# A scan and two MLPs on one core: running products stored ahead of block 1's rows and decays, rows in runs of 4 KB, GpSimd without splits and low parts

## The chip, the cores and the metric

The kernel runs on one core of a Trainium2 chip. A core has a matrix engine (TensorE, PE in the views), three engines for elementwise work (VectorE = DVE, ScalarE = ACT, GpSimd = POOL), a queue engine that issues DMA transfers (SyncE = SP), and 16 DMA engines that carry them. Each engine runs its own instructions in the order in which they are written and waits on semaphores for the others. The metric is the device time of one execution in microseconds (us); lower is better.

## The reference

A chunked linear scan (attention-like, with decays) feeds two MLPs one after the other. Shapes: 4 sequences, 8 heads, 768 positions, head width 32, state 16; the result is read as 3072 tokens of width 256, and both MLPs go from 256 to 2048 and back.

```python
# scan, for every chunk of positions
la = log(clip(a, 1e-6, 1));  cum = cumsum(la)
y  = ((C B^T) * exp(cum_i - cum_j) * causal) x  +  (C state) * exp(cum)
state = exp(sum(la)) * state + sum_j exp(cum_last - cum_j) B_j x_j
# first MLP, weights w_in, w_out
h = x @ w_in;  g = max(h, 0) + log1p(exp(-abs(h)));  x = g @ w_out
# second MLP
h = x @ w_in;  g = h if h >= 1, 0 if h <= -1, else (h + 1)^2 / 4;  out = g @ w_out
```

The weights of the MLPs come in 64-bit floats and the result is in 32-bit floats.

## The kernel before, in words

**Tiling.** The scan is cut into 6 chunks of 128 positions, called blocks 0 to 5, and each block into 4 units, one for each sequence: 24 units, u = 4c + b. A block of 4 units is 512 tokens, and one block is the moving side of the MLPs' products. A step s of the first MLP takes one slice of 128 hidden features (`fc`) of one block: `up` multiplies the block by the slice of w_in, ScalarE's softplus makes g from it, and `down` multiplies g by the slice of w_out into a running sum. Steps 0 to 3 take half a block and two slices each. Two consecutive slices need one piece of each weight: i2, o2 are the pieces of steps 4 and 5, i3, o3 those of 6 and 7, i4, o4 those of 8 and 9, and so on.

**Split numbers.** TensorE multiplies rounded 32-bit numbers quickly and unrounded ones slowly. So most factors are split into a high part (a cast, line 722) and a low part (the rest, by a subtraction: `split_w` at line 955 for weights, `g_lo` at 1424 for g). `up` makes three products for each of two halves of the depth (high x high, high x low, low x high: lines 1314 to 1316), `down` six for two output halves (1450). The first steps (`s < WHOLE`) are "whole": their `down` multiplies g and the weight unsplit (1438), and needs no `g_hi` and no `g_lo`, but takes TensorE longer for each product.

**Weights.** A piece of a 64-bit weight is 512 KB. It is loaded (`load_w`, line 769) into one of four buffers, and put together to 32 bits: `w0` and `w1` on ScalarE (785, 793; `w0` now and then on VectorE, 781), `w2` and `w3` on VectorE (805, 817), then the cast (722 or 724) and the subtraction (955).

**Decays.** For block 0 they are made by products. For blocks 1 to 5 the clipped `a` is stored once to DRAM (`clip_z`), and `rows` reads each pair of units back, broadcast to 128 partitions (line 1080, two transfers of 256 KB for a pair); VectorE's scan along the row then forms the running products (`decay`, line 1110). A second scan (`runs`, 1054) gives the running products from the start of each chunk. `store_runs` writes them to DRAM, one transfer for each block (1059), and `dec` reads a block's back, broadcast to 128 partitions (1087, 256 KB), for VectorE's multiplications (`cd`, 1130).

**What sets the order.** All of this is written as jobs with needs, costs for each engine that may run them, and buffers taken and given. A planner, `Jobs.order`, walks through time, gives each job to the engine on which it would end first (plus `BIAS`), sets the jobs of an engine one after another by due time, and has `RUSH` to shift single due times. Transfers are planned with a common pipe of `RATE` bytes per ns, and VectorE and GpSimd with a lock, since both are taken to hold each other up. The program then writes every engine's instructions in that order, so a change of a constant can move instructions everywhere. SyncE issues all transfers of this part of the program, one after another.

The scan's own products (lines 1152, 1201, 1223, 1255) stand between the steps of the first MLP, up to about 140 us; the second MLP ends the program.

Of the kernel before, what the change touches and what calls it, by code (L numbers as in the profile page):

```python
# [27 lines left out]
class Jobs:  # L28
# [18 lines left out]
    def order(self, slots, begin):  # L47
# [53 lines left out]
        for _ in range(len(jobs)):  # L101
            best = []
            for name in ready:
                options, _, _, takes, _, _ = jobs[name]
                got = pick(takes, min(at[name].values()))
                if got is None:
                    continue
                starts = {e: max(got[0], at[name][e], clock[e]) for e in options}
                bias = lambda e: BIAS_2 if e == POOL and name[0] == "split_w" and name[1] else BIAS.get(e, 0)
                _, start, engine = min((starts[e] + cost + bias(e), starts[e], e) for e, cost in options.items())  # L110
                best.append((start, due[name], number[name], name, engine, got[1]))
            assert best, [(name, jobs[name][3]) for name in ready]
# [13 lines left out]
            kind = name if isinstance(name, str) else name[0]  # L126
            if engine == POOL:

                begun = start + 60
                for a, b in locked:  # L130
                    if a < begun + cost and b > begun:
                        begun = b
                shared = [name, begun, begun + cost]
                cost += begun - start
            elif engine == DVE and kind in LOCKED:
                if shared and start < shared[2] and start + cost > shared[1]:
                    if start <= shared[1]:
                        late = start + cost - shared[1]
                        shared[1] += late
                        shared[2] += late  # L140
                        clock[POOL] = self.done[shared[0]] = shared[2]
                        self.end[shared[0]] += late
                        for other in after[shared[0]]:
                            if other in at:
                                for e in at[other]:
                                    at[other][e] = max(at[other][e], shared[2] + (80 if e == POOL else self.LATENCY[POOL]))
                    else:
                        cost += shared[2] - start
                locked = locked[-20:] + [(start, start + cost)]
# [90 lines left out]
def program():  # L240
# [30 lines left out]
        add(("rows_of", b), {DVE: 210, ACT: 200}, needs=["terms"] + [("columns", 1), ("rows_of", b - 1)] * (b == NB - 1), gives=["terms"] * (b == NB - 1))  # L271
    add("clip_load", SP, 400, due=-1e5, size=98e3)
    add("clip", DVE, 350, needs=["clip_load", ("columns", 1)] + [("rows_of", b) for b in range(NB - 1)])
    add("store", SP, 800, needs=["clip"], size=98e3)
    add("runs", DVE, 1500, needs=["clip", ("columns", 1)] + RUNS)
    for c in range(1, NC):
        add(("store_runs", c), SP, 600, needs=["runs"], size=16e3)
        add(("dec", c), SP, 400, needs=[("store_runs", i) for i in range(1, NC if c == 2 else 2)], takes=["dec"], size=262e3)
    for u in range(NU):
        c, b = divmod(u, NB)  # L280
        if u % 2 == 0:
# [2 lines left out]
        if c == 0:  # L284
            for hg in range(2):
                add(
                    ("spread", u, hg), PE, 470, needs=[("columns", hg), ("rows_of", u)] + ([("spread", u, 0)] if hg else []),
                    takes=[("acc", "h")] + [("ld", "lp")] * (hg == 0),
                )
                add(("decay", u, hg), ACT, 520, needs=[("spread", u, hg)], gives=[("part", ("spread", u, hg), 0)])  # L290
            decay = [("decay", u, 0), ("decay", u, 1)]
        else:
            if b % 2:
                add(("rows", u), SP, 1100, needs=["store"], takes=["lp"], size=524e3)
            add(("decay", u), DVE, 1130, needs=[("rows", pair_of(u))])
            decay = [("decay", u)]
            add(("cd", u), DVE, 200, needs=[("load", u), ("dec", c)])
# [79 lines left out]
    for m in range(2):  # L377
        for j in sorted(range(8), key=lambda j: first_use[m, j]):
            for kind in "io":
# [18 lines left out]
                w_made = ("s_sum", j) if m and kind == "i" else ("w2" if signed(*w) else "w3", *w)  # L398
                add(("w_hi", *w), {ACT: 520, DVE: 350}, needs=[w_made])
                if m == 0:  # L400
                    add(("split_w", *w), {DVE: 610, POOL: 1300}, needs=[("w_hi", *w)])
                    continue
                add(("w_lo", *w), DVE, 610, needs=[("w_hi", *w)])
                add(("put_w", *w), SP, 800, needs=[("w_lo", *w)], gives=[("w0", *w)] * (kind == "o"), size=524e3)
# [21 lines left out]
    for k, (m, p) in enumerate(GROUPS):  # L426
        done = finished(2 * p, 2 * p + 1) if m else [("ready", NU - 1)]
        done += [
            [], [("spill", i) for i in range(3)], [("p4", NFC * NC // 4 - 1)],
            [("fill", i) for i in range(3)],  # L430
        ][k]
        t = [("t_sum", k, i) for i in range(4)]
        sums = lambda n: {POOL: 1400 * n} if k in T_POOL else {DVE: 610 * n}
        add(t[0], sums(4), needs=done, takes=["w32"] * 3)
        add(t[2], sums(1), needs=[t[0]])
        add(t[1], sums(1), needs=[t[2]])
        add(t[3], sums(2), needs=[t[1], ("t_lo", k, 2)])
        for i in range(4):
            add(("t_hi", k, i), {POOL: 700, ACT: 520}, needs=[t[i]])
            add(  # L440
                ("t_lo", k, i), {POOL: 1500, DVE: 610}, needs=[("t_hi", k, i)] + [("t_lo", k, h) for h in (0, 1, 2) if i == 3],
                gives=[t[0]] * (i == 3),
            )


    for s, (m, c, t0, n, fc, m_fc) in enumerate(steps):
# [44 lines left out]
        if whole(s):  # L491
            needs = [("g", s)] + before + [("w2" if signed(0, "o", j) else "w3", 0, "o", j) for j in pieces]
            gives = [("g", s)]
        else:
            add(("g_hi", s), {ACT: 520, DVE: 360}, needs=[("g", s)], takes=["gh"])
            add(("g_lo", s), {DVE: 610, POOL: 1300} if s < GL_POOL else {DVE: 610}, needs=[("g_hi", s)], takes=["gl"], gives=[("g", s)])
            needs = [("g_lo", s)] + before + [("split_w", m, "o", j) for j in pieces]
            gives = [("g_hi", s), ("g_lo", s)]
        first = fc == 0 and t0 == 0
# [21 lines left out]


ORDER = [(0, 0, 0, 4), (0, 1, 0, 4), (0, None, 4, 12), (1, None, 0, 16)]
WHOLE = 8
ACT_UNTIL = 96
H_MORE = 16
H_ALL = 84
GL_POOL = 16
COLD = 0.0
KEEP = 26000.0  # L530
SIGNAL = 55.0
# [9 lines left out]
PRELU = (2, 2)  # L541
LOW_ACT = 1
PRE_FROM = 3
BIAS = {DVE: 400, POOL: 500}
PATIENCE = 0
EARLY = 30000.0
HASTE = 0
STAND_BY = 400
FAR = 10000.0
CHUNK = 9  # L550
BIAS_2 = 9000
RATE = 330.0
BEGIN = 14000.0
STRETCH = 1.0
LEAD = 2
# [10 lines left out]
N_G = 3  # L566
BEHIND = 500.0
RUSH = {
    ("decay", 2, 1): -8000, ("decay", 5): -16000, ("load_w", 1, "i", 2): -16000, ("w3", 0, "o", 4): 8000,
}  # L570
WARM = 10

# [5 lines left out]
def tile_kernel(ctx: ExitStack, tc: tile.TileContext, a0, al, bc, ub, w_in, w_out, w2_in, w2_out, out):  # L578
# [129 lines left out]
        return unit(*t_at[k][2 * (i - 1) + lo])  # L708


    clip_z = dram.tile([NU, 2, H * HALF], F32, name="clip_z")
    pre_w = {
        (kind, j, lo): dram.tile([128, 512], F32, name=f"pre_{kind}{j}{lo}") for kind in "io" for j in range(8) for lo in range(2)
    }
# [322 lines left out]
    def store(engine, *step):  # L1037
# [5 lines left out]
                queue = nc.scalar if len(parts_of) > 1 and i == 0 else nc.sync  # L1043
                queue.dma_start(out[steps[s][1], e, :, i * n:i * n + n], part[:, 0:n])
        else:
            nc.sync.dma_start(clip_z.rearrange("u s (h i) -> (u s) h i", h=H), z_t)

    @job
    def runs(engine):
# [5 lines left out]

    @job
    def store_runs(engine, c):
        n = NB * 2
        nc.sync.dma_start(clip_p[c].rearrange("h r i -> r h i"), tiles["clip"][c * n:(c + 1) * n])

    @job
    def load_bc(engine, v):
# [12 lines left out]
    @job  # L1075
    def rows(engine, u):

        t = flat(buf(*got["rows", u][0])).rearrange("p (u f) -> p u f", u=2)
        for s in range(2):
            nc.sync.dma_start(  # L1080
                t[s * HALF:(s + 1) * HALF], clip_z[u - 1:u + 1, s].unsqueeze(0).to_broadcast([HALF, 2, H * HALF])
            )

    @job
# [500 lines left out]
```

## Time and profile before

| | us |
|---|---|
| three runs | 555.36, 555.64, 560.16 |
| median | 555.64 |
| profiled execution | 557.88 |
| its span | 556.2 |
| granted TensorE clock in it | 1.00 (full) |

The profiled execution is one execution of its own, with the profiler on; its time is 1.7 us longer than its span, which runs from the first to the last instruction. The page and the answers that were read of it are shown further below. In a timeline the instructions of one engine overlap a little, since the next is begun before the last has ended: a "0.68" that is followed by another start 0.60 later takes 0.60 of the engine. "out<-in" gives the tile written and the tile read by the program's names, and a name after "<-" in brackets is the work whose end released the waiting instruction. A DMA share of 1 is all 16 DMA engines busy.

### The profile page before, as it was taken

The numbers are of one execution on the slowest core, as the hardware profiler recorded it, in microseconds if no ns is written. First come the engines' busy times: TensorE is split into PE (matmuls) and PEld (weight loads), VectorE is DVE, ScalarE is ACT, GpSimd is POOL, SyncE is SP. The second block draws the span as 40 slices with busy tenths as digits, with TensorE's granted clock in tenths as the row PEclk, the third lists the DMA queues.
The fourth block names the chain that finished last, engine by engine and source line by source line (L and its number), as shares of the span: only waits on it lengthen the run. The fifth ranks groups of instructions, "written<-read, shape, count | busy, mean of one in ns | idle before, by whom it ended". The sixth has DMA issues, their size and how long they took to land.

```text
span 556.2 us, 10449 instructions
## 1 busy us (share of the span) xinstructions
PE 546.8 (98%) x3994; PEld 442.3 (80%) x3994; DVE 435.7 (78%) x813; ACT 391.7 (70%) x720; POOL 39.2 (7%) x45
## 2 busy tenths in 40 slices
PE   9898999999999999999999999999999999999997
PEld 4765878878888888888888788888888888888885
DVE  6987999888865989876777898989886665876663
ACT  7968646645455666766566989786987875888773
POOL 3112220000000100001300000021310000000000
PEclk9999999999999999999999999999999999999999
DMA  8985467576242500276436314514100001100002
GB/s 280 392 220 178 138 194 210 165 235 183 93 165 75 180 1 1 96 258 205 143 113 214 128 59 152 171 56 130 62 1 0 1 1 38 39 0 1 1 1 76
DMA packets 34679, 64.73 MB, mean 116 GB/s; under 512 B 3684, under 2 KB 8164, under 8 KB 34628
## 3 DMA queue, kind: packets, MB, share of 16 engines
q1 hardware_dynamic: 34484, 63.93, 35.3%
q8 instruction: 31, 0.51, 0.4%
q14 instruction: 20, 0.16, 0.1%
q10 hardware_dynamic: 144, 0.13, 0.1%
HBM read 47.61 MB, written 16.43 MB: 115 GB/s over the span
## 4 chain that ended last, share of the span: by engine, by line
PE 87%; DMA 8%; DVE 2%; ACT 1%; SPq 1%; issue 1%; DVEq 0%; ACTq 0%
PE acc L1450 44%; PE h L1321 5%; PE h L1323 5%; PE h L1322 5%; PE z L1321 4%; PE z L1323 4%; PE z L1322 4%; PE h L1314 3%; PE h L1315 3%; PE h L1316 3%; DMA raw<-in_w_out_dram 2%; DMA ld<-clip_z 2%; DMA dec<-clip_p 2%; PE y L1223 1%; DMA st<-in_w_out_dram 1%; DMA u<-in_ub_dram 1%
## 5 line engine op out<-in xcount | busy, mean ns | idle before, releaser
L1424 DVE TENSOR_TENSOR gl<-g,gh 128x512 fp32r<-128x512 f32 x181 | 127.6, 709 | 55.1 <-PE acc L1450 31.0
L1450 PE MATMUL acc<-gh,woh 128*128 128x512 f32 x368 | 144.3, 392 | 0.0
L1450 PE MATMUL acc<-gh,wol 128*128 128x512 f32 x368 | 143.3, 389 | 0.0
L722 ACT CAST gh<-g 128x512 fp32r<-128x512 f32 x172 | 106.8, 621 | 26.4 <-PE acc L1450 14.2
L1450 PE MATMUL acc<-gl,woh 128*128 128x512 f32 x368 | 113.6, 389 | 0.0
L1450 PEld LDWEIGHTS acc<-gh,woh 128*128 128x128 f32 x368 | 69.1, 188 | 15.2 <-issue 0.5
L1450 PEld LDWEIGHTS acc<-gl,woh 128*128 128x128 f32 x368 | 69.1, 188 | 14.4
L1450 PEld LDWEIGHTS acc<-gh,wol 128*128 128x128 f32 x368 | 69.1, 188 | 14.1
L1409 ACT ACTIVATE g<-h 128x512 f32<-128x512 f32 x61 | 36.4, 597 | 51.7 <-PE h L1316 36.6
L1401 ACT ACTIVATE t<-t 128x512 f32<-128x512 f32 x96 | 60.9, 634 | 1.9
L1314 PE MATMUL h<-xh,wih 128*128 128x512 f32 (+1 forms) x114 | 46.0, 403 | 0.5 <-ACT wih L722 0.5
L1315 PE MATMUL h<-xh,wil 128*128 128x512 f32 (+1 forms) x114 | 42.9, 376 | 0.7 <-DVE wil L955 0.7
L1316 PE MATMUL h<-xl,wih 128*128 128x512 f32 (+1 forms) x114 | 42.9, 376 | 0.0
L1110 DVE TENSOR_TENSOR_SCAN ld<-ld,eye_t 128x512 f32<-128x512 f32 x20 | 25.1, 1289 | 4.0 <-DMA ld<-clip_z 2.7
L1394 ACT ACTIVATE t<-h 128x512 f32<-128x512 f32 x37 | 22.1, 598 | 7.8 <-PE h L1323 6.7
L1314 PEld LDWEIGHTS h<-xh,wih 128*128 128x128 f32 x114 | 21.4, 188 | 6.2 <-issue 1.1
L1413 DVE TENSOR_TENSOR g<-h,t 128x512 f32<-128x512 f32 x37 | 25.3, 685 | 1.1 <-ACT t L1401 0.3
L1394 ACT ACTIVATE t<-z 128x512 f32<-128x512 f32 x35 | 21.0, 599 | 7.1 <-DVE g L1413 3.9
L1315 PEld LDWEIGHTS h<-xh,wil 128*128 128x128 f32 x114 | 21.5, 188 | 5.6 <-DVE wil L955 1.0
L1413 DVE TENSOR_TENSOR g<-z,t 128x512 f32<-128x512 f32 x35 | 24.0, 686 | 1.5 <-ACT t L1401 0.5
L1316 PEld LDWEIGHTS h<-xl,wih 128*128 128x128 f32 x114 | 21.4, 188 | 4.0
L1409 ACT ACTIVATE g<-z 128x512 f32<-128x512 f32 x19 | 11.4, 598 | 17.4 <-PE z L1316 8.8
(320 smaller groups left out, 1008.0 us busy)
## 6 DMA issues: line engine op xcount, KB each, us to landing
st<-in_w_in_dram SPq DMA_DIRECT2D x15, 512.0 KB, 5.9
st<-in_w_out_dram SPq DMA_DIRECT2D x15, 512.0 KB, 6.7
u<-in_ub_dram SPq DMA_DIRECT2D x24, 256.0 KB, 6.2
ld<-clip_z SPq DMA_DIRECT2D x20, 256.0 KB, 6.0
bc<-in_bc_dram SPq DMA_DIRECT2D x12, 384.0 KB, 6.5
pre_i<-st_plain SPq DMA_DIRECT2D x15, 256.0 KB, 2.0
pre_s<-st_plain SPq DMA_DIRECT2D x14, 192.0 KB, 5.5
pre_o<-st_plain SPq DMA_DIRECT2D x10, 256.0 KB, 3.7
```

What stands on the lines that cost most here:

```text
L722: nc.scalar.copy(out, in_)
L1314: nc.tensor.matmul(o, wh, xh[c][:, k, t0:t0 + n], start=(k == 0), stop=False)
L1315: nc.tensor.matmul(o, wl, xh[c][:, k, t0:t0 + n], start=False, stop=False)
L1316: nc.tensor.matmul(o, wh, xl[c][:, k, t0:t0 + n], start=False, stop=(k == 1))
L1321: nc.tensor.matmul(bank, wh, bh, start=start, stop=False, skip_group_check=True)
L1322: nc.tensor.matmul(bank, wl, bh, start=False, stop=False, skip_group_check=True)
L1323: nc.tensor.matmul(bank, wh, bl, start=False, stop=True, skip_group_check=True)
L1401: nc.scalar.activation(out=t, in_=t, func=AF.Square, scale=0.5 / SAT, bias=0.5)
L1409: nc.scalar.activation(out=g, in_=ph, func=AF.Softplus)
L1413: nc.vector.tensor_tensor(out=g, in0=ph, in1=t, op=ALU.max)
L1424: engines[engine].tensor_tensor(out=mine("g_lo", s)[0], in0=mine("g", s)[0], in1=mine("g_hi", s)[0].bitcast(F32), op=ALU.subtract)
L1450: nc.tensor.matmul(acc_t(s, e), w, g[:, j * n:(j + 1) * n], start=(begins(e, j) and g is gh and i == 0), stop=(fc + j == NFC - 1 and g is ...
```

## The change

- `WHOLE` goes from 8 to 6: steps 6 and 7 are split like all later ones, with `g_hi` and `g_lo` jobs of their own.
- GpSimd no longer gets subtractions of the kinds `split_w`, `g_lo` and `t_lo`, nor casts `t_hi` (the set `POOLED` is empty). 25 jobs leave it: 5 `split_w`, 3 `g_lo` and 12 `t_lo` go to VectorE, 5 `t_hi` to ScalarE. With the `g_lo` of steps 6 and 7, VectorE has ten subtractions more in the first 100 us.
- `clip_z` is laid out so that the two units of a pair lie behind each other; each partition's row is read as one piece of 4 KB instead of two of 2 KB. `COPIES = 1` keeps one copy.
- `store_runs` is two transfers for each block instead of one, ten in all instead of five.
- The planner's costs and rates for `rows`, `store_runs` and `dec` grow, its lock is modelled otherwise, and `RUSH` has other entries.

The core of the diff:

```diff
-                bias = lambda e: BIAS_2 if e == POOL and name[0] == "split_w" and name[1] else BIAS.get(e, 0)
+                bias = lambda e: BIAS.get(e, 0)
...
-                begun = start + 60
-                for a, b in locked:
-                    if a < begun + cost and b > begun:
-                        begun = b
-                shared = [name, begun, begun + cost]
+                begun = max([b for a, b in locked if a < start + 60 < b], default=start + 60)
+                shared = [name, begun, begun + cost, False]
...
-    add("store", SP, 800, needs=["clip"], size=98e3)
+    add("store", SP, 400 * COPIES, needs=["clip"], size=98e3 * COPIES)
...
-        add(("store_runs", c), SP, 600, needs=["runs"], size=16e3)
-        add(("dec", c), SP, 400, needs=[("store_runs", i) for i in range(1, NC if c == 2 else 2)], takes=["dec"], size=262e3)
+        add(("store_runs", c), SP, 700, needs=["runs"], size=16e3)
+        add(("dec", c), SP, 400, needs=[("store_runs", i) for i in range(1, NC if c == 2 else 2)], takes=["dec"], size=262e3 * 1.5)
...
-                add(("rows", u), SP, 1100, needs=["store"], takes=["lp"], size=524e3)
+                add(("rows", u), SP, 1100, needs=["store"], takes=["lp"], size=524e3 * SLOW)
...
-                    add(("split_w", *w), {DVE: 610, POOL: 1300}, needs=[("w_hi", *w)])
+                    add(("split_w", *w), {POOL: 1300} if ("split_w", *w) in POOLED else {DVE: 610}, needs=[("w_hi", *w)])
...
-            add(("t_hi", k, i), {POOL: 700, ACT: 520}, needs=[t[i]])
+            add(("t_hi", k, i), {ACT: 520}, needs=[t[i]])
...
-            add(("g_lo", s), {DVE: 610, POOL: 1300} if s < GL_POOL else {DVE: 610}, needs=[("g_hi", s)], takes=["gl"], gives=[("g", s)])
+            add(("g_lo", s), {POOL: 1300} if ("g_lo", s) in POOLED else {DVE: 610}, needs=[("g_hi", s)], takes=["gl"], gives=[("g", s)])
...
-WHOLE = 8
+WHOLE = 6
...
-BIAS = {DVE: 400, POOL: 500}
+BIAS = {DVE: 600}
+POOLED = set()
...
-BIAS_2 = 9000
-RATE = 330.0
+RATE = 370.0
+COPIES = 1
+SLOW = 1.75
...
-    ("decay", 2, 1): -8000, ("decay", 5): -16000, ("load_w", 1, "i", 2): -16000, ("w3", 0, "o", 4): 8000,
+    ("decay", 2, 1): -4000, ("decay", 5): -16000, ("load", 17): 8000, ("rows", 9): -4000, ("w0", 0, "i", 4): 16000,
...
-    clip_z = dram.tile([NU, 2, H * HALF], F32, name="clip_z")
+    clip_z = dram.tile([COPIES, 2, NU, H * HALF], F32, name="clip_z")
...
-        n = NB * 2
-        nc.sync.dma_start(clip_p[c].rearrange("h r i -> r h i"), tiles["clip"][c * n:(c + 1) * n])
+        for s in range(2):
+            r = s * NU + c * NB
+            nc.sync.dma_start(clip_p[c].rearrange("h (b s) i -> s b h i", s=2)[s], tiles["clip"][r:r + NB])
...
-                t[s * HALF:(s + 1) * HALF], clip_z[u - 1:u + 1, s].unsqueeze(0).to_broadcast([HALF, 2, H * HALF])
+                t[s * HALF:(s + 1) * HALF].rearrange("p u f -> p (u f)"),
+                clip_z[:, s, u - 1:u + 1].rearrange("k u f -> k (u f)").unsqueeze(1).to_broadcast(
+                    [COPIES, HALF // COPIES, 2 * H * HALF]
+                ),
```

The order moves at three places. On SyncE, from o4's weight to the decays (`st_136` to `st_139` are the four weight buffers, `ld_121` and `ld_122` the rows of two pairs, `dec_134` and `dec_135` the two decay slots), before:

```order
L769 DMA st_139<-in_w_out_dram 128x2x512
L1080 DMA ld_122<-clip_z 64x2x512 x2
L1080 DMA ld_121<-clip_z 64x2x512 x2
L1059 DMA clip_p<-more_148 8x8x64 x5
L769 DMA st_136<-in_w_in_dram 128x2x512
L769 DMA st_137<-in_w_out_dram 128x2x512
L769 DMA st_138<-in_w_in_dram 128x2x512
L1087 DMA dec_134<-clip_p 128x1x512
L1087 DMA dec_135<-clip_p 128x1x512
L769 DMA st_139<-in_w_out_dram 128x2x512
```

and with the change:

```order
L1079 DMA ld_122<-clip_z 64x1x1024 x2
L1079 DMA ld_121<-clip_z 64x1x1024 x2
L1058 DMA clip_p<-more_148 4x8x64 x2
L766 DMA st_139<-in_w_out_dram 128x2x512
L1058 DMA clip_p<-more_148 4x8x64 x8
L766 DMA st_136<-in_w_in_dram 128x2x512
L766 DMA st_138<-in_w_out_dram 128x2x512
L1089 DMA dec_134<-clip_p 128x1x512
L1089 DMA dec_135<-clip_p 128x1x512
L766 DMA st_137<-in_w_in_dram 128x2x512
L766 DMA st_139<-in_w_out_dram 128x2x512
```

The load of o4 stood ahead of the rows and now stands behind them and two of the ten stores; i6, which stood ahead of both decays, now stands behind them, and the second decay is block 3's.

On ScalarE, around the rebuild of i5 and the steps behind it (lines 793 and 790 are `w1`, 785 and 782 `w0`, 722 and 719 the cast, 1409 and 1411 the softplus; names `g` and `gh` are reused buffers), before:

```order
L722 CAST woh_93<-w_482 128x512
L1409 ACTIVATE gh<-h_208 128x512
L722 CAST wih_78<-w_566 128x512
L722 CAST woh_94<-w_586 128x512
L1409 ACTIVATE gh<-h_210 128x512
L793 ACTIVATE t<-st_136,low_bias 128x512
L785 ACTIVATE w_566<-st_136 128x512
L793 ACTIVATE t<-st_137,low_bias 128x512
L785 ACTIVATE w_586<-st_137 128x512
L1409 ACTIVATE gh<-h_208 128x512
L793 ACTIVATE g<-st_138,low_bias 128x512
```

and with the change:

```order
L790 ACTIVATE t<-st_136,low_bias 128x512
L719 CAST wih_78<-w_545 128x512
L1411 ACTIVATE g<-h_210 128x512
L790 ACTIVATE g<-st_138,low_bias 128x512
L719 CAST gh<-g 128x512
L782 ACTIVATE w_603<-st_138 128x512
L719 CAST woh_94<-w_603 128x512
L1411 ACTIVATE g<-h_208 128x512
L719 CAST gh<-g 128x512
L790 ACTIVATE t<-st_137,low_bias 128x512
L1411 ACTIVATE g<-h_210 128x512
L782 ACTIVATE w_669<-st_137 128x512
```

The cast of `wih_78`, the weight piece i4 of steps 8 and 9, stood ahead of the rebuild of `st_136` and now stands behind its `w1`. The g of step 6 goes to `g`, with a cast to `gh`, and that cast stands behind the `w1` of o5 (`st_138`).

On TensorE, the end of step 7's `up` and what follows it (`h` is the bank of `up`, `acc` the running sums), before:

```order
L1316 MATMUL h_208<-xl_360,wih_77 128x512
L1438 MATMUL acc_285<-gh,w_482 128x512
L1438 MATMUL acc_270<-gh,w_482 128x512
L1314 MATMUL h_210<-xh_359,wih_78 128x512
L1315 MATMUL h_210<-xh_359,wil_86 128x512
L1316 MATMUL h_210<-xl_360,wih_78 128x512
L1314 MATMUL h_210<-xh_359,wih_78 128x512
L1315 MATMUL h_210<-xh_359,wil_86 128x512
L1316 MATMUL h_210<-xl_360,wih_78 128x512
L1438 MATMUL acc_285<-gh,w_482 128x512
L1438 MATMUL acc_270<-gh,w_482 128x512
```

and with the change:

```order
L1318 MATMUL h_208<-xl_360,wih_77 128x512
L1316 MATMUL h_210<-xh_359,wih_78 128x512
L1317 MATMUL h_210<-xh_359,wil_86 128x512
L1318 MATMUL h_210<-xl_360,wih_78 128x512
L1316 MATMUL h_210<-xh_359,wih_78 128x512
L1317 MATMUL h_210<-xh_359,wil_86 128x512
L1318 MATMUL h_210<-xl_360,wih_78 128x512
L1452 MATMUL acc_285<-gh,woh_93 128x512
L1452 MATMUL acc_285<-gh,wol_101 128x512
L1452 MATMUL acc_270<-gh,woh_93 128x512
L1452 MATMUL acc_270<-gh,wol_101 128x512
```

Step 8's `up` (with `wih_78`) stood behind the whole down of step 6 and now stands ahead of that down, which is split.

## Rows read from the trace of the kernel before

**Rows 1.** The page, part 1: busy us, share of the span, instructions.
```profile
PE 546.8 (98%) x3994; PEld 442.3 (80%) x3994; DVE 435.7 (78%) x813; ACT 391.7 (70%) x720; POOL 39.2 (7%) x45
```

**Rows 2.** Stretches: length, busy PE, PEld, DVE, ACT, POOL; PEclk, DMA share, GB/s.
```profile
100.00:160.00 60.00, 60.00 (x1100) 48.59 (x1099) 52.28 (x117) 32.05 (x67) 0.00 (x0) 1.00 0.55 172
...
300.00:540.00 240.00, 239.83 (x1058) 198.12 (x1057) 183.58 (x298) 193.94 (x344) 12.18 (x10) 1.00 0.15 52
```

**Rows 3.** Waits of TensorE, 0 to 100 us: total, times, longest.
```profile
PE acc L1438 <- ACT gh L1409: 2.1, 2, 1.5
...
PE y L1223 <- DVE ld L1166: 0.8, 1, 0.8
```

**Rows 4.** Timeline of TensorE: start, us, instruction, [idle before <- releaser].
```profile
33.69 1.88 PE L1438 MATMUL acc<-gh,w 128*128 128x512 f32 x4
...
35.63 0.39 PE L1315 MATMUL h<-xh,wil 128*128 128x512 f32 x1
...
39.90 1.88 PE L1438 MATMUL acc<-gh,w 128*128 128x512 f32 x4
...
43.72 1.98 PE L1438 MATMUL acc<-gh,w 128*128 128x512 f32 x4 [0.55 <-ACT gh L1409]
...
47.63 0.50 PE L1314 MATMUL h<-xh,wih 128*128 128x512 f32 x1 [0.53 <-ACT wih L722]
48.78 0.50 PE L1315 MATMUL h<-xh,wil 128*128 128x512 f32 x1 [0.66 <-DVE wil L955]
```

**Rows 5.** The chain of waits, 0 to 80 us: start, us, what.
```profile
3.48 5.80 DMA st<-in_w_in_dram
...
26.32 9.42 DMA ld<-clip_z
...
55.74 1.36 PE acc L1450 x6
```

**Rows 6.** Timeline of SyncE's queue: issue, us, transfers.
```profile
9.30 0.37 SPq L769 DMA_DIRECT2D raw<-in_w_out_dram  x1
...
34.25 0.41 SPq L769 DMA_DIRECT2D st<-in_w_in_dram  x1
35.13 0.40 SPq L769 DMA_DIRECT2D st<-in_w_out_dram  x1
35.81 0.37 SPq L769 DMA_DIRECT2D st<-in_w_in_dram  x1
```

**Rows 7.** Timeline of VectorE.
```profile
45.42 0.90 DVE L1130 TENSOR_TENSOR u<-u,dec 128x128 f32<-128x128 f32 x4 [4.70 <-DMA dec<-clip_p]
```

**Rows 8.** Timeline of ScalarE.
```profile
37.94 0.76 ACT L793 ACTIVATE t<-st,low_bias 128x512 uint32<-128x512 uint32 x1 [0.35 <-DMA st<-in_w_in_dram]
...
41.88 0.76 ACT L793 ACTIVATE t<-st,low_bias 128x512 uint32<-128x512 uint32 x1 [2.61 <-DMA st<-in_w_out_dram]
```

**Rows 9.** Stretches about the rows and dec.
```profile
22.00:28.00 6.00, 6.00 (x44) 5.73 (x43) 5.83 (x8) 5.35 (x13) 1.56 (x2) 1.00 1.05 389
28.00:33.40 5.40, 5.40 (x26) 4.60 (x25) 4.17 (x9) 4.29 (x8) 1.42 (x1) 1.00 1.04 219
41.00:45.50 4.50, 3.95 (x13) 2.00 (x11) 0.08 (x1) 3.48 (x6) 0.00 (x0) 1.00 0.80 218
```

**Rows 10.** VectorE by line, 0 to 100 us: busy us, mean ns | idle before.
```profile
L1110 DVE TENSOR_TENSOR_SCAN ld<-ld,eye_t 128x512 f32<-128x512 f32 x12 | 15.6, 1341 | 2.4 <-DMA ld<-clip_z 2.4
L805 DVE SCALAR_TENSOR_TENSOR w<-w,t 128x512 uint32<-128x512 uint32 x13 | 9.9, 759 | 2.0 <-ACT w L785 1.2 <-ACT w L783 0.4 <-ACT t L793 0.2
L1424 DVE TENSOR_TENSOR gl<-g,gh 128x512 fp32r<-128x512 f32 x10 | 7.8, 790 | 0.2 <-ACT gh L722 0.2
L817 DVE SCALAR_TENSOR_TENSOR w<-st,w 128x512 uint32<-128x512 uint32 x10 | 7.7, 781 | 0.0
...
L955 DVE TENSOR_TENSOR wil<-w,wih 128x512 fp32r<-128x512 f32 x7 | 4.8, 682 | 0.0
```

**Rows 11.** The page, part 5: the scan over the whole span.
```profile
L1110 DVE TENSOR_TENSOR_SCAN ld<-ld,eye_t 128x512 f32<-128x512 f32 x20 | 25.1, 1289 | 4.0 <-DMA ld<-clip_z 2.7
```

More of the change, by code (lines that the diff above doesn't have):

```diff
@@ L136, in order @@
                 if shared and start < shared[2] and start + cost > shared[1]:
-                    if start <= shared[1]:
+                    if start <= shared[1] and not shared[3]:
                         late = start + cost - shared[1]
-                        shared[1] += late
-                        shared[2] += late
+                        shared[1:] = shared[1] + late, shared[2] + late, True
                         clock[POOL] = self.done[shared[0]] = shared[2]
@@ L438, in program @@
         for i in range(4):
-            add(("t_hi", k, i), {POOL: 700, ACT: 520}, needs=[t[i]])
+            add(("t_hi", k, i), {ACT: 520}, needs=[t[i]])
             add(
-                ("t_lo", k, i), {POOL: 1500, DVE: 610}, needs=[("t_hi", k, i)] + [("t_lo", k, h) for h in (0, 1, 2) if i == 3],
+                ("t_lo", k, i), {POOL: 1300} if ("t_lo", k, i) in POOLED else {DVE: 610}, needs=[("t_hi", k, i)] + [("t_lo", k, h) for h in (0, 1, 2) if i == 3],
                 gives=[t[0]] * (i == 3),
@@ L527 @@
 H_ALL = 84
-GL_POOL = 16
 COLD = 0.0
@@ L1045, in store @@
         else:
-            nc.sync.dma_start(clip_z.rearrange("u s (h i) -> (u s) h i", h=H), z_t)
+            for i in range(COPIES):
+                nc.sync.dma_start(clip_z[i].rearrange("s u (h i) -> (s u) h i", h=H), z_t)
     @job
@@ L1551 @@
     c6 = C.reshape(NB, H, NC, Q, N)
-    al = np.ascontiguousarray(a.reshape(NB, H, NC, 2, HALF).transpose(2, 0, 3, 1, 4)).reshape(NC * NB * 2, H * HALF)
+    al = np.ascontiguousarray(a.reshape(NB, H, NC, 2, HALF).transpose(3, 2, 0, 1, 4)).reshape(NC * NB * 2, H * HALF)
     a0 = np.ascontiguousarray(a6[:, :, 0]).reshape(NB * H, Q)
```

## The prediction, made before the changed kernel was run

> **What bounds the kernel now.** The busy line comes first: TensorE works 98% of the span [rows 1]. A mean over a span hides stages, so the second view is the table of stretches [rows 2]: TensorE is busy in every microsecond from 100 to 160 us and in 239.83 of 240 from 300 to 540, at the full granted clock, while VectorE (183.58 of 240) and ScalarE have room. Time can only be won there by giving TensorE less to do, or in the first 100 us by removing its waits. The list of waits of that stretch [rows 3] has 2.1 us for g from ScalarE and 0.8 for ld from VectorE, and its timeline [rows 4] shows 0.53 and 0.66 more at 47.63 and 48.78 us. That is 4.1 us of waits for what the change moves. With the matmuls that it saves (0.7, below), 4.8 us could be won in all. A measurement of this kernel can tell about 1% from no change, 5.6 us, so a gain that large is nearly excluded before anything is costed. A loss isn't: every new wait in this dense stretch counts in full.
>
> The chain of waits [rows 5] and SyncE's timeline [rows 6] show what feeds the stretch. The weight of 3.48 us lands at 3.48 + 5.80 = 9.28, and the ninth transfer issued from it on is issued at 9.30. Likewise the block-1 rows hold the queue: the last of four lands at 26.32 + 9.42 = 35.74 and the next issue begins at 35.81. I read this as eight transfers outstanding on SyncE, the next waiting for the oldest.
>
> **The change part by part.** *Whole downs.* Steps 6 and 7 lose the four unsplit products. From the start at 33.69 to the product at 35.63 is 1.94 us; less the 0.23 of the product between, a whole down takes 1.71. A split one takes 1.36 [rows 4, 5]. Two steps: 2 x (1.71 - 1.36) = **-0.7 us**.
>
> *Waits that go.* VectorE sits 4.70 us before its first multiplication by dec [rows 7], and behind it stand the rebuild of block weights and the subtractions that TensorE waits for at 43.72, 47.63 and 48.78: 0.55 + 0.53 + 0.66 [rows 4]. In the new order those weights stand elsewhere, so I drop all three: **-1.7 us**. Bounds: 0 if they only change place, -2.5 if ld's 0.8 [rows 3] goes too.
>
> *Rows in runs of 4 KB, with o4's weight behind them.* (iN and oN are pieces N of the first MLP's two weights.) Without that weight's 512 KB ahead the rows land 0.5 / 0.389 = 1.3 us sooner, near 34.4. For the length of the runs two rows give bounds: 389 GB/s while weights and other loads are moved, 219 while rows are mainly moved [rows 9]. 1 MB takes 2.7 us at the one and 4.8 at the other, so longer runs are worth 0 to -2.1 us of landing time. I take 0: both stretches have runs of 2 KB or thereabouts, so it is the source, one short tensor read 64 times, that differs. The Trainium skill (DMA: Bandwidth & Descriptors, Specifications) asks for at least 512 B per transfer for full rate; by that, 2 KB was long enough and 4 KB brings nothing. The trace agrees that run length alone isn't the price, with 389 against 219 at equal runs. The scan at 35.99 isn't what TensorE waits for, so sooner rows buy TensorE nothing directly.
>
> *What the queue then does.* This is the new cost. Ten stores of running products stand where five did, with o4's weight after the second. The tenth store is the eighth issue behind that weight, and so waits for its landing: 1.3 us behind the rows at 34.4 gives 35.7 to 35.9. The weight i5 is issued at 36.3 instead of 34.25 [rows 6]. Before, it was used at 37.94 less the 0.09 of handing over: 3.6 us after issue [rows 8]. So it lands at 39.9. ScalarE then rebuilds it (0.67 to the next instruction) and only then casts the weight of step 8 (0.62), which the new order puts behind it. Step 8's first product, now ahead of down 6 and so due at 39.90 [rows 4], starts at 41.2: **1.3 us**, and 0.4 more before its second product, which needs VectorE's 0.61 subtraction behind the cast: 1.7. Bounds 0 (weight as early as before) and 2.4 (o4 lands only when the rows did before). Down 6 then needs g_hi, behind o5's rebuild on ScalarE. That weight took 41.8 - 35.1 = 6.7 us [rows 6, 8]; issued at 36.7 it is there at 43.4, the cast ends 43.4 + 0.67 + 0.62 = 44.7, and step 8's products end near 44.4: **0.3**; upper bound 1.2, when dec, which one multiplication ahead of g_lo 6 on VectorE waits for, arrives at 45.42 as before. Last, i6 is fetched behind both decs, and ScalarE's rebuild of it stands ahead of the g of the step after: **1.0**, an estimate by half of what dec keeps VectorE waiting less two steps of cover (4.70/2 - 1.36); bounds 0 and 2.0. Together **+3.0**, from 0 to +5.6.
>
> *GpSimd gives its splits away.* Before 100 us VectorE takes ten more subtractions of 0.61 (its steps apart; 682 ns each with overlap): 6.1 us. Against it stands what sharing with GpSimd cost: the twelve scans of L1110 took 1341 ns, all twenty 1289, so the other eight (20 x 1289 - 12 x 1341) / 8 = 1211; the low parts of g (L1424) 790 against the 682 of L955, the two rebuilds 759 and 781 against the same [rows 10, 11]. 12 x 0.13 + 10 x 0.11 + 13 x 0.08 + 10 x 0.10 = 4.7 us. The 1.4 left over I cost at **0**: VectorE's 4.70 us before dec [rows 7] hide it; without that cover it is 1.4. GpSimd itself is in no wait of rows 3 and 4. The later low parts, twelve of 0.61 on VectorE and five casts on ScalarE, lie where VectorE has 56 of 240 us free: 0, with 7.3 us of VectorE as the price if it were full.
>
> Sum: -0.7 - 1.7 + 3.0 = **+0.6 us**. The profiled run took 557.88 us (span 556.2), so 558.5 for it; it lies 2.24 over the median of the runs, which I take as scatter. Against the median, 555.64 + 0.6 = **556.2 us**.
>
> **The rivals.**
> *A. The weights come in time.* If rows land at the lower bound (-2.1), o4, i5 and what follows are issued as early as before, and the new waits vanish. For it: nothing in the rows says that the 219 is the source rather than the runs. Against it: the queue order. Gain 0.7 + 1.7 = 2.4, with ld's 0.8 gone 3.2: 552.4 to 553.2, **552.8**. Chance 0.25.
>
> *B. The decs block more than I charge.* The window before dec's arrival at 45.4 moves 218 GB/s at a DMA share of 0.80 [rows 7, 9]. If both decs use half the DMA engines, 256 KB cost 1.35 us each instead of 0.67, i6 is held longer, and down 8 waits at its upper bound: +2.5 to +4.9, **559 to 560.5**. The share of 0.80 speaks against it, because half the engines would show 0.5, unless another transfer fills the others. Chance 0.15. The Trainium skill (DMA: Bandwidth & Descriptors, Why a DMA increments its semaphore by 16 and not by 1) has the transfer spread over the largest divisor, up to 16, of the slowest dimensions; dec's source has 8 heads outermost, which would make it 8.
>
> *C. The other side: 4 KB reads of the same 4 KB are slower, not faster.* All 64 partitions read one line; if longer pieces collide more and a block's rows take 8 us instead of the 5.4 of 28.00 to 33.40, VectorE's scans, which already wait 2.4 us for clip_z [rows 10], stand in blocks 1 to 5, some 1.5 to 2 us each: 555.64 + 0.6 + 6 to 9 = **562 to 565**. It decides from a transfer of about 8 us on, where cover in the dense stretch (VectorE 52.28 of 60) runs out. Chance 0.07.
>
> *D. The change doesn't do what it says:* the decay fetched "sooner" is issued at 37 us after all, behind ten stores. This is inside my forecast.
>
> **How the numbers follow.** Forecast 0.53, A 0.25, B 0.15, C 0.07. Predicted is the forecast's 556.2. The range takes the forecast with all bounds: low -0.7 - 1.7 - 0.8 + 0 = -3.2, 552.5; high -0.7 + 0 + 5.6 = +4.9, 560.5. It covers A and B and leaves C out. Faster by over 1% (below 550.1) needs more than the waits there are: 0.03, for something not in these rows. Slower by over 1% (above 561.2) is C and a little of B's end: 0.10. Within 1%: 0.87.
>
> **What would show it.** Right: SyncE's issue of i5 near 36.3 instead of 34.25; a wait before step 8's first product of over 1 us, with ScalarE's cast as releaser; no wait of L1438 at 43; VectorE's L1110 at 1.21 instead of 1.34 us; rows landing at 34 or later. Wrong: rows landing near 32 (A), a wait of VectorE on clip_z of more than 5 us (C), idle of TensorE behind 100 us from VectorE's or ScalarE's new low parts, which I cost at nothing, or a granted clock below 1.00.

## The result, and the profile after

The changed kernel took 560.14 us (median of 16 runs), the kernel before 557.20 (16 runs, its first three among them): a ratio of 1.0052, 95% interval 1.0033 to 1.0071, which is 2.9 us more (1.8 to 4.0). That lies within 1%, inside the range, and above the 556.2 that I had forecast, or 557.8 if the forecast's +0.6 is set on the median of 557.2.

The profiled execution took 560.20 us, its span is 558.5. The page's first line, as in [rows 1]:

```profile
PE 548.1 (98%) x4000; PEld 443.2 (79%) x4000; DVE 437.8 (78%) x827; ACT 397.4 (71%) x735; POOL 5.8 (1%) x20
```

TensorE is as full as before. GpSimd's 39.2 us are 5.8. The waits of TensorE in the first 100 us, as in [rows 3]:

```profile
PE y L1159 <- DMA bc<-in_bc_dram: 2.5, 1, 2.5
PE acc L1452 <- ACT gh L719: 1.3, 1, 1.3
...
PE acc L1452 <- DVE gl L1426: 0.4, 1, 0.4
PE acc L1440 <- ACT gh L1411: 0.3, 1, 0.3
```

None of the waits that I took away is left: no whole down (L1438, now L1440) waiting at 43 us, no wih, no wil, no ld. But the longest one is new and stands where I had looked at nothing: 2.5 us at 5 to 8 us, for bc, the B and C of the first units. The stretches behind it (columns as in [rows 2]):

```profile
8.00:10.00 2.00, 2.00 (x18) 0.90 (x14) 0.00 (x0) 0.00 (x0) 0.00 (x0) 0.57 0.97 349
10.00:12.00 2.00, 2.00 (x7) 0.93 (x6) 0.60 (x1) 1.21 (x3) 0.42 (x2) 0.57 1.06 407
```

After that wait the granted clock is 0.57 for 4 us: for most of them TensorE runs at the lower of its two levels, 1.2 GHz. Up to the issue of bc at 2.08 us SyncE does the same in both kernels, and this has to be put aside before anything else can be read from the two traces; the first two experiments do that.

SyncE's queue, as in [rows 6]:

```profile
27.30 2.55 SPq L1058 DMA_DIRECT2D clip_p<-more  x2
30.94 0.41 SPq L766 DMA_DIRECT2D st<-in_w_out_dram  x1
32.09 5.12 SPq L1058 DMA_DIRECT2D clip_p<-more  x8
37.32 0.40 SPq L766 DMA_DIRECT2D st<-in_w_in_dram  x1
...
39.69 0.38 SPq L766 DMA_DIRECT2D st<-in_w_in_dram  x1
```

In both kernels the stores stand behind block 1's rows and ahead of the decays; the title has them ahead of the rows, which they are not. o4's weight is issued at 30.94, eight more stores hold the queue for 5.12 us, and i5 goes out at 37.32 instead of 34.25. Behind both decays i6 follows at 39.69, where it was 35.81. VectorE's work by form, as in [rows 10]:

```profile
L1112 DVE TENSOR_TENSOR_SCAN ld<-ld,eye_t 128x512 f32<-128x512 f32 x12 | 14.1, 1211 | 0.4 <-DMA ld<-clip_z 0.2
L1426 DVE TENSOR_TENSOR gl<-g,gh 128x512 fp32r<-128x512 f32 x16 | 11.0, 685 | 1.7 <-ACT gh L719 1.6
L802 DVE SCALAR_TENSOR_TENSOR w<-w,t 128x512 uint32<-128x512 uint32 x11 | 7.6, 687 | 1.3 <-ACT w L780 0.7 <-ACT w L782 0.6
```

The scan takes 1211 ns instead of 1341, the low parts 685 instead of 790, the rebuild 687 instead of 759, the figures from which I had costed GpSimd's part.

### The profile page after: what moved, and what is told of

It reads as the page before. It is cut to its first block, busy times and chain, and to the rows that moved or that the text cites. A ratio compares the mean times of both kernels' runs of the same rounds, so it can differ in the third digit from the quotient of the medians.

```text
span 558.5 us, 10424 instructions
## 1 busy us (share of the span) xinstructions
PE 548.1 (98%) x4000; PEld 443.2 (79%) x4000; DVE 437.8 (78%) x827; ACT 397.4 (71%) x735; POOL 5.8 (1%) x20
## 4 chain that ended last, share of the span: by engine, by line
PE 91%; DMA 3%; ACT 3%; DVE 2%; issue 1%; SPq 1%; ACTq 0%
PE acc L1452 44%; PE h L1323 5%; PE h L1324 5%; PE h L1325 5%; PE z L1323 4%; PE z L1324 4%; PE z L1325 4%; PE h L1316 4%; PE h L1317 4%; PE h L1318 4%; DMA st<-in_w_in_dram 2%; PE y L1225 1%; PE acc L1440 1%; DMA bc<-in_bc_dram 1%; PE y L1257 1%; PE z L1317 1%
## 5 line engine op out<-in xcount | busy, mean ns | idle before, releaser
L1452 PE MATMUL acc<-gh,woh 128*128 128x512 f32 x372 | 146.1, 393 | 1.3 <-ACT gh L719 1.3
L1452 PE MATMUL acc<-gh,wol 128*128 128x512 f32 x372 | 144.9, 389 | 0.0
L719 ACT CAST gh<-g 128x512 fp32r<-128x512 f32 x175 | 108.6, 620 | 25.3 <-PE acc L1452 15.2
L1452 PE MATMUL acc<-gl,woh 128*128 128x512 f32 x372 | 114.9, 389 | 0.4 <-DVE gl L1426 0.4
L1112 DVE TENSOR_TENSOR_SCAN ld<-ld,eye_t 128x512 f32<-128x512 f32 x20 | 23.5, 1211 | 1.3 <-DMA ld<-clip_z 1.1
```

The source lines that it names most:

```text
L719: nc.scalar.copy(out, in_)
L1452: nc.tensor.matmul(acc_t(s, e), w, g[:, j * n:(j + 1) * n], start=(begins(e, j) and g is gh and i == 0), stop=(fc + j == NFC - 1 and g is ...
```

## The experiments

Ratios are to the kernel before, run on the same chip in turn with each kernel; one per mille is 0.56 us. e1 and e2 are single runs and have no ratio.

| kernel | ratio | 95% interval |
|---|---|---|
| the change | 1.0052 | 1.0033 to 1.0071 |
| e3 stores late, o4 early | 1.0050 | 1.0031 to 1.0070 |
| e4 before + whole layout | 1.0037 | 1.0023 to 1.0051 |
| e5 ScalarE's order | 1.0050 | 1.0033 to 1.0066 |
| e6 before + 4 KB runs, five stores | 0.9990 | 0.9970 to 1.0010 |
| e7 before + ten stores | 1.0026 | 1.0013 to 1.0039 |
| e8 before, GpSimd freed | 1.0062 | 1.0045 to 1.0078 |
| e9 the change, five stores | 1.0002 | 0.9986 to 1.0019 |
| e10 e9 + second decay late | 1.0001 | 0.9986 to 1.0016 |
| e11 e10 + ScalarE's order | 0.9987 | 0.9971 to 1.0004 |

### Both kernels again (e1, e2)

No edit. Expected of the kernel before:

> The kernel before, unchanged, for a second trace. Scatter theory: the late landing of the first bc (7.69 us in the changed kernel's trace, 5.30 in this one's, with the same instructions up to it) is a matter of the single execution, and can show here as well; then TensorE waits up to 2.5 us for bc at 5 to 8 us. Change theory: here it lands near 5.3 us again.

and of the changed one:

> The changed kernel, unchanged, for a second trace. Scatter theory: the first bc lands near 5.3 us in this execution or another; then the queue's delay (i5 issued at 36 to 37 us) is no longer covered by a late start, and TensorE's waits between 40 and 52 us grow to 3 us or more. Change theory: bc lands near 7.7 us again, the granted clock falls to 0.57 in 8 to 12 us, and the waits stay at some 2 us.

TensorE's waits of the kernel before, first 100 us of this execution:

```profile
PE acc L1438 <- ACT gh L1409: 2.0, 1, 2.0
...
PE y L1223 <- DVE ld L1166: 0.8, 1, 0.8
PE h L1315 <- DVE wil L955: 0.7, 1, 0.7
PE y L1157 <- DMA bc<-in_bc_dram: 0.3, 1, 0.3
PE h L1314 <- ACT wih L722: 0.2, 1, 0.2
```

and of the changed kernel:

```profile
PE h L1316 <- ACT g L1411: 1.9, 1, 1.9
PE y L1225 <- DVE ld L1168: 1.3, 1, 1.3
...
PE acc L1440 <- ACT gh L1411: 0.4, 1, 0.4
```

bc is waited for 0.3 us in the one and not at all in the other. So the 2.5 us are not in every execution of the change. Over all the traces of this study that wait is none and 0.3 us in the two of the kernel before, 0.4 and 0.2 in e6 and e8, which are made from it and keep its five stores, 0.7, 1.8 and 1.1 in e9 to e11, and 2.5, none, 0.3, 0.9, 1.4 and 1.0 with ten stores (the change, e2, e3, e4, e5, e7). Of the last nine only e2 and e3 wait as little as the first four, so a part of the late start may go with the kernel; thirteen traces can't settle it. The 16 runs of each kernel spread over 4.8 and 3.6 us. Why the landing varies is open.

These two make a clean pair: spans of 555.4 and 557.3, 1.9 us apart. With the start undisturbed, the wait that I had predicted is there; at 1.9 us it is shorter than the 3 us expected of e2. TensorE in the changed kernel (timeline, as in [rows 4]):

```profile
42.50 0.50 PE L1316 MATMUL h<-xh,wih 128*128 128x512 f32 x1 [1.87 <-ACT g L1411]
...
43.50 0.63 PE L1316 MATMUL h<-xh,wih 128*128 128x512 f32 x1
```

and ScalarE beside it:

```profile
40.70 0.76 ACT L790 ACTIVATE t<-st,low_bias 128x512 uint32<-128x512 uint32 x1 [3.40 <-DMA st<-in_w_in_dram]
41.36 0.60 ACT L719 CAST wih<-w 128x512 fp32r<-128x512 f32 x1
41.87 0.59 ACT L1411 ACTIVATE g<-h 128x512 f32<-128x512 f32 x1
```

ScalarE sits 3.40 us until i5 lands, rebuilds it, and only then casts i4's weight and makes step 6's g, for which step 8's first product waits 1.87 us. What I had not seen comes next: from 43 us on a product that takes 0.23 from start to start takes 0.43. The stretches:

```profile
43.00:44.00 1.00, 1.00 (x5) 0.75 (x4) 0.28 (x1) 1.00 (x3) 0.00 (x0) 0.54 0.61 160
44.00:45.00 1.00, 1.00 (x4) 0.80 (x3) 0.96 (x3) 1.00 (x3) 0.00 (x0) 0.50 0.65 233
45.00:46.00 1.00, 1.00 (x3) 0.77 (x3) 1.00 (x4) 0.81 (x2) 0.00 (x0) 0.50 1.05 393
46.00:47.00 1.00, 1.00 (x5) 0.75 (x4) 1.00 (x3) 0.22 (x1) 0.00 (x0) 0.75 0.48 180
```

The granted clock is at its lower level, 0.50, until 46.5: 0.46 + 0.50 + 0.50 + 0.25 = 1.7 us of full speed lost, nearly as much as the wait itself. The sums for the pair: waits 4.0 in the first 100 us before (the rows above; the one left out is 1.1 us ahead of the first product, the same in both) and 3.6 + 0.5 (near 229 us, below) = 4.1 after; the clock +1.7; the two whole downs -0.7, as the prediction has them; two more idle products (fillers that compute nothing) at 15 us, 2 x 0.23 = +0.5. Together +1.6 of the 1.9.

### Stores late (e3)

```diff
 result = jobs.order(slots, {...})
+ load_w o4 moved ahead of the first rows; store_runs 3 moved ahead of the second dec;
+ store_runs 2, 4, 5 moved ahead of load_w i6
```

> The changed kernel with only SyncE's order changed: o4's weight ahead of block 1's rows as in the kernel before, and the stores of blocks 2 to 5 behind the weights i5 and o5. Queue theory (my prediction's new cost, 3.0 us): i5 is issued near 34.3 us instead of 37.3, TensorE's waits of 40 to 52 us shrink, and the time falls by 1.5 to 3 us against the changed kernel, to about the kernel before's (0 to +1 us). Rival, the cost lies elsewhere (at the start or behind 100 us): no more than 0.5 us below the changed kernel, +2.4 or more against the kernel before.

i5 went out at 30.5 us, even earlier than expected, and the time stayed: 1.0050. The wait had moved (waits of TensorE, 0 to 100 us):

```profile
PE acc L1452 <- ACT gh L719: 1.4, 1, 1.4
```

The 1.4 us are down 8 at 47 us: its g_hi stands on ScalarE behind the rebuild of i6, and i6 now stands behind the decays and eight stores, and was issued at 43.05. Ten stores in the queue delay whatever follows them; moved, they delay the next weight. My expectation for the queue theory failed: the trace shows the wait moved, not removed.

### The layout alone, the runs alone, the stores alone (e4, e6, e7)

e4 is the kernel before with the diff's hunks on `clip_z`, `store_runs`, `rows` and `al`, and no other. e6 has the order block, half, sequence, so that a pair is 4 KB in one piece and a block still one store; e7 only cuts the stores in two:

```diff
 # e6
-    clip_z = dram.tile([NU, 2, H * HALF], F32, name="clip_z")
+    clip_z = dram.tile([NC, 2, NB, H * HALF], F32, name="clip_z")
-    clip_z[u - 1:u + 1, s].unsqueeze(0).to_broadcast([HALF, 2, H * HALF])
+    clip_z[u // NB, s, u % NB - 1:u % NB + 1].rearrange("u f -> (u f)").unsqueeze(0).to_broadcast([HALF, 2 * H * HALF])
 # e7
-    nc.sync.dma_start(clip_p[c].rearrange("h r i -> r h i"), tiles["clip"][c * n:(c + 1) * n])
+    for i in range(2): # rows i * NB to (i + 1) * NB of the block
+        nc.sync.dma_start(...)
```

> The kernel before, in its own order, with only the layout of the change: rows in runs of 4 KB and ten stores of running products instead of five. Runs theory (2 KB was long enough): the rows take as long as before, 9.1 to 9.4 us from issue to landing, and the time is +0 to +1 us, from five more issues in the queue. Rival A (4 KB lifts the rows to 389 GB/s): rows land 2 us sooner, -0.5 to -1.5 us. Rival C (4 KB reads of one line are slower): rows land over 2 us later, +3 us or more.

> The kernel before with the rows in runs of 4 KB and nothing else: the stored order is block, half, sequence, so a block's running products are still one store and there are five. All other instructions stand as before. Runs theory (2 KB was long enough): rows land within 0.5 us of before, time -0.7 to +0.7 us. Rival A: -0.5 to -1.5 us by sooner rows. Rival from the run with the layout alone: the 2 us it lost were the runs', +1.5 to +3 us.

> The kernel before with each store of running products cut in two and nothing else. Store theory: ten issues hold SyncE's queue, i5 is issued at 38 us or later instead of 34.3 to 34.9, step 9's weight and its low part come later, and the time is +1 to +2.1 us. Rival (the layout run lost at its start, by scatter): +0 to +0.5 us.

The whole layout costs 2.1 us (1.3 to 2.8), more than the +1 that I had allowed it; the runs alone cost -0.6 (-1.7 to +0.6), the stores alone 1.5 (0.7 to 2.2). e6's time would fit rival A as well, but its rows took 10.0 to 10.4 us from issue to landing, against 9.4 to 10.0 and 8.9 to 9.6 in the two traces of the kernel before: they came no sooner. So runs of 4 KB change nothing that can be measured, and by the runs the layout's cost is its second half, the doubled stores. In SyncE's queue of e7:

```profile
27.55 9.40 SPq L1059 DMA_DIRECT2D clip_p<-more  x10
37.07 0.41 SPq L769 DMA_DIRECT2D st<-in_w_in_dram  x1
```

ten stores hold it from 27.55 to 36.95, and i5 is issued at 37.07 (34.25 and 34.90 in two traces of the kernel before). In e7's profile the start was late as well: 1.0 us for bc, and then the products of L1157 took 629 ns in the median, 374 in e1, though the granted clock reads 1.00 in those rows. Both kernels have the same order on TensorE and ScalarE, so their timelines can be laid side by side. The rebuild of i5 and the whole down of step 6, in e1:

```profile
39.19 0.76 ACT L793 ACTIVATE t<-st,low_bias 128x512 uint32<-128x512 uint32 x1 [1.19 <-DMA st<-in_w_in_dram]
...
40.31 1.88 PE L1438 MATMUL acc<-gh,w 128*128 128x512 f32 x4
```

and in e7:

```profile
41.07 0.75 ACT L793 ACTIVATE t<-st,low_bias 128x512 uint32<-128x512 uint32 x1 [1.46 <-DMA st<-in_w_in_dram]
...
41.92 1.88 PE L1438 MATMUL acc<-gh,w 128*128 128x512 f32 x4
```

TensorE is 1.61 us late by then, the weight 1.88, and TensorE's wait for the cast of i5, 0.2 in e1 (above), is in e7:

```profile
PE h L1314 <- ACT wih L722: 0.4, 1, 0.4
```

The late start covers the late weight, so that profile can't show the cost of the queue by itself. The 1.5 us stand on the runs. That an undisturbed start would pay up to the 1.88 us of the late weight is an estimate, and near them.

### ScalarE's order (e5)

```diff
+ w_hi i4, g 6, g_hi 6 moved ahead of w1 i5 (ScalarE)
+ split_w i4, g_lo 6 moved ahead of w0 i5 (VectorE)
```

> The changed kernel with five instructions moved ahead on two engines: on ScalarE the cast of i4, the g and the g_hi of step 6 ahead of the first rebuild of i5, on VectorE the low parts of i4 and of step 6's g ahead of the rebuild of i5 that waits for its landing. My theory (step 8's products wait because the cast stands behind a weight that lands near 40.6 us): the 1.9 us wait at 40 us goes, and with it the half clock of 43 to 46.5 us (1.6 us); 2 to 3.6 us less than the changed kernel, within 1 us of the kernel before. Rival (the queue is the bound): the same time is waited at the next weight or dec, 43 to 50 us, and the time falls by less than 1 us.

The rival was right: 1.0050. The wait at 40 us is gone, and the clock stays at 1.00 from 40 to 54 us, but the time went elsewhere (waits of TensorE):

```profile
PE acc L1452 <- ACT gh L719: 2.0, 1, 2.0
...
PE acc L1440 <- ACT gh L1411: 1.3, 2, 1.0
...
PE h L1316 <- ACT g L1411: 0.9, 1, 0.9
```

2.0 us is down 8 again, behind i6; the 0.9 stands at 44 us before step 9's first product, behind ScalarE's rebuild of o5. In this execution the start took another 1.4 for bc. Which weight ScalarE serves first changed where the time was lost, and not how much.

### Five stores in the changed kernel (e9 to e11)

e9 is the change with e6's layout, so with five stores; e10 also moves the second dec behind o6; e11 adds e5's moves.

> The changed kernel with five stores of running products instead of ten (rows kept in 4 KB runs; the stored order is block, half, sequence), all else in its order. Store theory (ten stores alone cost 1.5 us): -1 to -2 us against the changed kernel, +1 to +2 against the kernel before; i5 is issued 1 to 2 us earlier than at 36.3. Rival (what stays is the queue behind the rows and decs): under 0.7 us less than the changed kernel.

> As the last, and the second decay (block 3's) is fetched behind o6 instead of ahead of i6. Theory (down 8's wait, 1.3 to 2.1 us in three traces, is i6 behind the decays): i6 lands 0.7 to 1.4 us earlier and that wait shrinks by as much; -0.5 to -1.5 us against the last. Rival (i6's buffer is free only when i4 is rebuilt, so i6 can't come earlier): no difference beyond 0.4 us.

> As the last, with the five instructions of ScalarE and VectorE moved as in the run of that order. Theory (each of the three repairs takes away one wait: the store queue, i6, the cast behind i5): no wait of TensorE above 1 us between 38 and 52 us, full clock, and the time 0.5 to 2 us below the kernel before. Rival (the transfers of the first 45 us as a whole bound TensorE, whoever is served first): the waits move on, and the time stays at +1 us or more against the kernel before.

e9 undoes the whole loss: 1.0002. It went further than the store theory expected (+1 to +2). SyncE's queue:

```profile
28.27 0.40 SPq L766 DMA_DIRECT2D st<-in_w_out_dram  x1
...
34.34 0.41 SPq L766 DMA_DIRECT2D st<-in_w_in_dram  x1
```

i5 is issued at 34.34, where it was before the change, though o4 still stands behind the first store. SyncE's own waits, 20 to 46 us, show the difference, in e2 with ten stores (L1058 is a store):

```profile
SPq L1058 <- DMA ld<-clip_z: 3.2, 4, 0.9
```

and in e9 with five (L766 is a weight):

```profile
SPq L766 <- DMA ld<-clip_z: 1.6, 2, 0.9
```

In e2 four stores wait for the four row transfers, the last until 34.9 us, and three more stores go out ahead of i5, at 36.30. In e9 i5 itself waits for a row transfer. TensorE's waits are:

```profile
PE y L1225 <- DVE ld L1168: 1.4, 1, 1.4
...
PE acc L1452 <- ACT gh L719: 1.0, 1, 1.0
PE h L1323 <- DVE h L1366: 0.5, 1, 0.5
```

Step 8 waits for nothing; down 8 waits 1.0 us for its g_hi. With the second dec out of i6's way (e10) that wait is gone from the list:

```profile
PE y L1159 <- DMA bc<-in_bc_dram: 1.8, 1, 1.8
...
PE h L1323 <- DVE h L1366: 0.5, 1, 0.5
```

In time, e10 can't be told from e9, nor e11 from either: a wait of 1.0 us is gone from the trace, and the times can't tell the theory's 0.5 to 1.5 us from the rival's 0.4 or less. In e11's trace the clock is full and no wait of 38 to 52 us is above 1.0, as expected, but 1.0 us stands before step 9's first product, as in e5, and 0.9 before a whole down at 25 us. Of e11's expectation (0.5 to 2 us below the kernel before) the median lies at -0.7 and the interval includes zero; its rival's +1 is excluded. That is a version that beats the change by 3.6 us, each measured against the kernel before, and the kernel before not demonstrably.

### GpSimd freed in the kernel before (e8)

```diff
-                    add(("split_w", *w), {DVE: 610, POOL: 1300}, needs=[("w_hi", *w)])
+                    add(("split_w", *w), {DVE: 610}, needs=[("w_hi", *w)])
 # likewise g_lo, t_lo {DVE: 610} and t_hi {ACT: 520}
```

> The kernel before with GpSimd's splits, low parts and casts of that kind given to VectorE and ScalarE, ordered anew by the planner. Theory (VectorE's scans fall to 1.21 us and pay for the added subtractions): -1 to +1 us. Rival (VectorE is too full): +1.5 us or more, with TensorE's waits on VectorE over 3 us in the first 100 us.

1.0062: 3.5 us slower (2.5 to 4.4), the rival's size. Two waits stand for it, the second at 392 us:

```profile
PE y L1223 <- DVE ld L1166: 2.6, 1, 2.6
...
PE z L1321 <- DVE z L1364: 0.9, 1, 0.9
```

and behind the first the clock falls (stretches):

```profile
71.00:74.00 3.00, 0.45 (x9) 0.05 (x11) 3.00 (x11) 0.00 (x0) 0.00 (x0) 1.00 1.04 277
74.00:76.00 2.00, 2.00 (x129) 1.83 (x130) 2.00 (x7) 0.27 (x1) 0.00 (x0) 0.55 0.63 244
76.00:78.00 2.00, 2.00 (x6) 1.60 (x7) 2.00 (x7) 1.97 (x7) 0.00 (x0) 0.60 0.05 11
```

VectorE is busy for all of 71 to 78 us, and ld comes late in the order that the planner made of the jobs. The change has given the same jobs away and has no wait for ld at 70 to 80 us in any trace, and e9, with GpSimd freed too, runs in the time of the kernel before. That speaks for the order as e8's price, and against the jobs' sum; no run changes e8's order alone.

## Why the prediction was right, point by point

- **The bound.** TensorE had at most 4.8 us to win, and nothing was won. The forecast's side of the 1% holds. Its middle doesn't: +2.9 was measured where +0.6 was summed, and only the upper bounds of the terms take that in.
- **Whole downs, -0.7.** Nothing in the traces contradicts it, and no run isolates it.
- **Waits that go, -1.7.** They are gone from the traces of the change, the 0.8 for ld at 78 us too, and of 2.0 for g at 18 us (e1) 0.4 are left. But as many came, which the prediction had only as a bound: ld at 17 us (1.3 in e2, 1.4 in e9), down 8's, 0.5 near 229 us. In sum 4.0 before and 4.1 after, and still 4.5 in e9, where the ten stores are gone.
- **What the queue then does, +3.0: the mis-sized step.** The chain was as told up to its last link. i5 was issued at 36.30 in e2 (36.3 predicted), its rebuild began at 40.70 (landing predicted at 39.9), and step 8 waited 1.9 us (1.7), though for step 6's g, which stands behind the cast, and not for the cast. What the term lacked is the clock: 1.7 us more behind that wait. Down 8's wait for i6 (1.0 predicted) is 1.3 in the profile of the change, 1.0 in e9 and 2.0 in e5; in e2, where step 8 waits, it is none. By the runs the five stores more cost 2.8 us (1.0052 against 1.0002). I had put the delay down to o4's weight behind two stores, for which the tenth store waits. In e2 that store does go out right behind o4's landing, at 35.90, but the ninth had only just been issued. e7 has the delay with o4 ahead of the rows, and e9 has none with o4 behind a store: it takes the ten stores, whose later ones wait for the rows up to the last, and not o4's place.
- **Runs, 0.** Right: e6. Of the two bounds, 0 and -2.1, the first holds. The Trainium skill (DMA: Bandwidth & Descriptors, Specifications) asks for no more than 512 B, and e6 agrees: 2 KB was long enough.
- **GpSimd, 0.** The durations came out as worked out (1211 against 1.21; 685). The 0.5 us near 229 us, TensorE waiting for VectorE's h (in the lists of e9 and e10 above), I take for the price of the later low parts that I had put at nothing: every trace of the changed order has it and none of the kernel before or of those made from it.
- **The signs.** Two that I had named for being wrong are there: that idle time behind 100 us, and a granted clock below 1.00, in both traces of the change. In the first of them step 8 waits for nothing; its loss is bc's wait and the clock behind it, which are in no term. That its time lies in the range is in part luck.
- **The rivals.** A (rows sooner, 0.25): the last rows landed at 35.7 and 34.9 us in the two traces of the change, 35.7 and 35.9 in those of the kernel before; no gain. B (i6 behind the decays, 0.15; its lower end should read 558.1, 555.64 + 2.5): the measured 560.14 lies in its range, but its mechanism isn't what cost it, since e9 keeps both decays ahead of i6 and loses nothing. Its wait is real, 1 to 2 us, and moving one decay ends it. Its condition has support in the traces: each dec transfer posts 9 updates of its landing where a weight or a row posts 16. What that costs no run isolates. C (slower runs): excluded by e6. D: the decay came a little sooner for VectorE, at 45.1 and 44.0 us against 45.4 and 44.7, though it is issued later; VectorE waits 1.28 us for it in the first trace of the change instead of 4.70, being busier until then.

What stays open: the pair of traces shows +1.9 and the runs +2.9 (1.8 to 4.0). Whether the rest is the executions' scatter at the start or something that the changed kernels do there, these traces can't tell. That five stores end the loss is shown by the runs of e9; the path from the stores to TensorE is seen in one undisturbed trace, e2.

## What to carry to other kernels

Count the transfers of a queue, not only their bytes: small stores that stand behind large loads hold up every later issue (here ten of 8 KB in place of five of 16 KB moved i5's issue by some 2 us and the time by 1.5 to 2.8), and reordering them here only chose which weight was late. Cost a wait of a dense TensorE with what its clock may lose behind it. Before two traces are compared, take each a second time and look at the first 10 us.

## What the runs showed of the hardware

The clock did not fall behind every wait. It fell to 0.50 to 0.64 in the rows behind waits of 1.9 us (e2), 2.5 (the change's start), 2.6 (e8) and 3.2 (e4, at 19 us), and stayed at 1.00 behind 2.0 us at 18 to 20 us in e1 (rows below) and 2.0 at 48 to 50 in e5:

```profile
18.00:20.00 2.00, 0.03 (x4) 0.00 (x0) 1.97 (x5) 1.97 (x4) 0.00 (x0) 1.00 1.04 400
20.00:22.00 2.00, 2.00 (x10) 1.79 (x11) 1.44 (x4) 2.00 (x7) 0.00 (x0) 1.00 1.05 397
```

So length alone doesn't decide in these traces. In e7 the products behind the 1.0 us for bc ran as slowly as those of the change at 0.50 (0.63 us, and 0.60 to 0.64 there) while the row reads 1.00, so the row may miss a fall; in e1 and e5 the products behind the two waits of 2.0 us kept their usual pace. A scan of 128x512 on VectorE took 1211 ns with GpSimd nearly idle and 1341 with GpSimd at 18 us of the 100, and the rebuilds and low parts 9 to 13% less. e8, the kernel before with those jobs taken from GpSimd, has the same durations (1210 and 681): the gain from an idle GpSimd is as large as it was worked out to be, and bought nothing here. The rows' stretch, 28.00 to 33.40, moved 219 GB/s in the kernel before, in runs of 2 KB, and 231 in e6, in runs of 4 KB, with the DMA engines full in both (share 1.04).
